# Routed attention and a gated spectral convolution: three-bank transposes, sums split between VectorE and GpSimd, and a new order of work

## The chip, the cores and the metric

The kernel runs on one core of a Trainium2 chip. The core has five engines that each work through a queue of their own in order: TensorE (PE in the profile; its weight loads are listed as PEld), VectorE (DVE), ScalarE (ACT), GpSimd (POOL) and SyncE (SP), which here only issues DMAs. They wait for each other through semaphores. Matrix products land in PSUM, eight banks of 128 partitions by 512 f32; all else lies in SBUF. The metric is the device time of one execution, the median of several.

## The reference

The first half is attention with a mask by clusters, for 4 batches, 8 heads, 768 positions and 64 columns per head. Each query and each key is assigned to one of 16 centroids of its head, and a query sees only the keys of its own centroid:

```
q_assign = argmax(q_n @ c_n.T)          # per head, over 16 centroids
k_assign = argmax(k_n @ c_n.T)
mask     = q_assign[:, None] == k_assign[None, :]
scores   = where(mask, q @ k.T / 8, -1e9)
attn     = softmax(scores)              # over the keys
x        = (attn @ v) with the heads side by side   # 768 x 512 per batch
```

The second half, per batch, multiplies two projections of `x` with a long convolution of the third, done in the frequency domain:

```
x1, x2, x3 = split(x @ w_proj)
x2_conv    = irfft(rfft(x2) * rfft(filter))     # along the 768 positions
out        = (x1 * x2_conv * x3) @ w_out
```

## The kernel before, in words

Attention goes by pairs of heads. There are 16 pairs (`n` is a group of two pairs, `NG` = 8; `pr` the pair in it), and each pair runs over six chunks `sk` of 128 keys. A chunk has 768 queries of two heads, so 1536 columns of scores, made in thirds of 512 columns (`THIRDS`): a score product into one PSUM bank (`sc`), an exponential on ACT into one of five buffers `p` (`exp`, lines 669 and 672). Then the chunk's product with the values is added into the pair of banks 4 and 5, `pair` (`pv`, line 683, f32), and the chunk's exponentials are added on VectorE into `acc` (line 697), whose sum over partitions gives the softmax denominators. The first sum of a pair takes chunks 0 and 1 together, the other four one chunk each, all 128x1536 f32. When the pair is done ACT copies `pair` to `osb` (line 701). The denominators of the middle ten pairs are reduced by three DMAs on GpSimd's queue that add one half of the partitions of `acc` onto the other (line 731), then go through DRAM (`dd`, `dp`, `dn`, `dr`) and return broadcast as `rb`; those of the first four pairs and of the last two use a product with ones on PE (`den`, line 711). Line 777 multiplies `osb` with `rb` into `xT`.

Ahead of a group, `routing` prepares its scores. The raw q and k (`qkraw`, six tiles of 128x128 f32 for a pair's q or k) are transposed on PE. From the third group on (`n > 1`), six transposes go into two banks in one go (`tr2`, line 556), and two copies of 384 columns bring them to `qkT`; the first two groups do three transposes per bank (line 566). The copies may go to ACT or VectorE (line 261 if ACT, line 263 if VectorE or GpSimd, both in the helper `copy`). `qkT` is cast to bf16 into `aug` (64x768, four casts for a pair), multiplied with the centroids (`sim`, line 586), transposed back (line 599), and VectorE makes one-hot rows of the nearest centroid (lines 607 to 624). These return through a transposing DMA as extra rows of `aug` (line 462), so that the score product itself carries the mask.

After every two groups a batch's `hyena` runs: the projection of x2 (line 809), a sum and a difference on VectorE (line 822), the spectrum (through `columns`), its products with the filter's spectrum from PSUM (`tm`, line 833), sums of those into `y` (line 837), the two other projections (`G`) with their product on VectorE (line 873), the inverse transform (`I`), its sums and differences into `sd` (line 898), their last sums into `yy`, called folds here (line 908), the product with the gate into `y2` (line 911), and the output projection (`W`), whose PSUM results are copied to `ob` and stored. For the first three batches this lies among the next attention groups, for the last it is the end of the kernel. On PE, `product` issues a 128-column product either whole (line 72) or as two halves of 64 columns (line 74), whichever keeps the array at the width of the instruction before.

The order of all this is not written by hand. Each step is an `op` with the engines that it may go to and a cost for each, a due time, what it reads and writes, and the banks that it takes and frees. `Plan.place` lists them: at each step it takes, of the engines' ready steps, the one that can start first, and among those within 0.1 us the one with the earliest due time; at most four banks may be held by scores, and at most four by other work, while scores last (`HELD`). A step marked `lock` on VectorE and one on GpSimd are never put beside each other. `NUDGE` adds a shift to the due time of single steps, by their number. The result is one fixed order on each engine; on the chip only the semaphores decide when each instruction starts.

The lines that say how a step meets its engine are few:

```
op(("DVE", 1.75), acc, due + .2 - 40 * (last and sk == NT - 1), ..., w=[("acc", os)], lock=True)
op({"POOL": 1.45, "DVE": .68} if last and i < 2 else ("DVE", .68), ...)      # y
op(("DVE", .55), fold, due + 2, ...)
op(("DVE", .95), ..., op=Alu.mult), due + 2.5, ...)                          # y2
```

Of the kernel before, what the change touches and what calls it, by code (L numbers as in the profile page):

```python
# [34 lines left out]
ROWS = 16  # L35
# [5 lines left out]
NUDGE = {6:-0.2,9:0.7,10:3.7,11:-0.3,71:-0.3,75:-1.5,90:7.4,91:7.4,129:-0.8,140:0.4,152:2.6,155:-6.2,156:6.6,158:-2.3,167:0.6,169:-4.1,187:-5.6,193:0.1,204:0.1,207:-0.7,209:0.8,212:-0.2,216:15.5,218:8.0,222:-3.8,228:-3.1,238:-1.7,239:-1.7,240:-1.7,243:1.1,245:-2.9,253:-4.1,255:-7.1,256:-7.1,257:-3.0,264:4.3,274:2.3,281:0.9,288:9.1,289:11.6,298:0.6,322:-4.8,328:-9.2,329:-0.5,343:0.7,363:0.5,368:-1.5,369:-1.5,370:0.7,371:-1.5,375:0.1,378:0.5,379:0.7,390:-1.8,391:-0.1,400:-0.2,406:2.8,409:-4.8,410:0.5,416:0.2,418:-1.0,433:-11.9,434:0.6,440:-3.7,479:0.8,480:-0.3,481:-0.5,485:1.1,494:-0.6,495:-4.2,504:2.3,508:-1.9,511:-0.2,517:-0.3,518:-5.0,523:-0.4,524:0.5,526:2.1,539:-2.3,547:0.2,554:10.5,558:0.3,565:-0.3,568:1.6,573:0.4,587:-4.9,590:0.2,595:-17.3,597:-2.4,617:0.7,620:-1.0,631:0.3,634:2.8,646:0.7,658:0.8,664:0.1,665:-1.9,684:2.2,690:-8.8,693:2.2,698:0.1,703:-7.8,704:-1.7,705:-1.7,729:0.5,740:1.0,750:-0.6,759:0.5,767:0.4,779:-0.7,782:1.7,784:-0.1,788:0.7,789:-0.3,790:0.8,800:2.5,805:-3.5,810:1.5,822:0.1,824:0.1,826:-0.5,828:-0.3,843:-8.5,848:-1.7,861:0.5,870:2.5,871:2.5,872:-1.3,883:-5.3,888:-3.6,897:-0.8,898:-1.1,901:-3.5,915:-3.1,926:4.0,936:-4.1,937:-3.0,940:2.9,941:0.4,947:-0.4,949:-0.6,969:-0.8,981:1.0,996:2.0,997:2.0,999:-0.3,1026:2.7,1029:-2.1,1031:0.1,1036:3.2,1039:2.0,1043:-1.2,1048:1.2,1050:-0.1,1054:-1.5,1056:10.8,1062:0.4,1066:0.9,1077:-7.7,1083:-3.4,1092:-0.1,1098:-1.0,1101:0.3,1116:-6.9,1118:-4.2,1122:2.8,1123:2.4,1124:2.4,1127:1.5,1130:-1.5,1131:0.3,1132:-2.9,1143:-2.6,1150:4.6,1157:-0.6,1194:-0.9,1236:-2.9,1253:-0.5,1255:0.7,1257:0.7,1263:0.3,1270:-0.2,1271:-1.1,1276:-3.6,1285:2.1,1286:4.6,1295:4.9,1311:-2.5,1317:-2.0,1321:0.4,1322:0.7,1332:-1.9,1337:-0.6,1351:5.6,1357:0.2,1359:0.5,1363:-0.5,1373:-1.5,1374:1.1,1381:0.2,1383:-0.3,1414:-2.7,1419:-0.5,1422:0.3,1425:0.7,1441:9.4,1450:3.5,1461:2.0,1478:-1.3,1479:3.3,1500:1.2,1501:-8.3,1521:0.2,1529:0.8,1546:0.2,1551:-0.2,1552:-1.1,1555:1.4,1557:0.1,1563:-0.6,1591:0.2,1600:-0.4,1619:-4.8,1624:2.8,1630:-1.5,1634:0.3,1640:-4.0,1641:-4.0,1642:-13.7,1643:-4.0,1655:-4.1,1657:0.4,1666:0.5,1672:1.9,1677:-0.3,1680:2.8,1681:2.8,1682:2.8,1685:-2.9,1697:-0.5,1713:-7.0,1741:5.6,1747:13.3,1764:1.1,1771:-3.3,1774:3.4,1776:0.2,1788:-7.8,1797:0.1,1808:-0.1,1809:-0.1,1814:-4.0,1817:-2.0,1823:3.3,1827:-0.7,1841:-1.3,1844:0.9,1859:2.4,1862:2.5,1863:2.1,1865:-0.3,1870:-0.4,1887:2.4,1890:3.2,1898:-7.4,1901:-0.8,1902:-1.5,1903:-0.8,1904:-0.8,1905:-1.8,1906:-1.8}  # L41
# [35 lines left out]
class Plan:  # L77
# [35 lines left out]
    def place(self, free0, banks_for, switch=0.1, wait=0.1, rate=215e3, bonus=10.84378, margin=0.02195, shape=1.63806):  # L113
# [57 lines left out]
        for o in self.ops:  # L171
            if not o.left:
                enqueue(o)
# [70 lines left out]
def build(T):  # L244
# [33 lines left out]

    def dma(e):
        return (T.nc.scalar if e == "ACT" else T.nc.sync).dma_start  # L280
# [4 lines left out]
    EV384 = {"ACT": .48, "DVE": .55}  # L285
# [89 lines left out]
    def tables(got):  # L375
# [44 lines left out]
        for i in range(3):  # L420
# [7 lines left out]
            for n, (row, c0, c1, cs) in enumerate(terms):  # L428
# [9 lines left out]
                op(("DVE", .68), lambda e, i=i, row=row, c0=c0, t=t, h=hs[1 - cs]: T.nc.vector.scalar_tensor_tensor(  # L438
# [28 lines left out]
    def first_masks(pr):  # L467
# [4 lines left out]
        for ch in range(2):  # L472
# [6 lines left out]
            op(("PE", .67), sim, due + .1 * ch, r=[("qkT", z, ch) for z in (2 * pr, 2 * pr + 1)] + ["cbd"], w=[h],  # L479
# [57 lines left out]
    def routing(n):  # L537
# [5 lines left out]
        for u in range(8):  # L543
# [7 lines left out]
            if n > 1 and ch == 0:  # L551
                h = Bank(cls, 2)

                def tr2(e, s=s, h=h):
                    for i in range(NT):
                        T.nc.tensor.transpose(bank(h.ids[i // 3])[:, ts(i % 3, 128)], raw(s, i), T.ident)  # L556
                op(("PE", .68), tr2, due, r=[("qkraw", s, 0), ("qkraw", s, 1), "ident"], w=[h], alloc=h)
                for c in range(2):
                    op(EV384, lambda e, z=z, c=c, h=h: copy(e, T.qkT[z][:, c], bank(h.ids[c])[:, :384]), due + .9,
                       r=[h], w=[("qkT", z, c)], free=[h])  # L560
            elif n < 2:
                h = Bank(cls)

                def tr(e, s=s, ch=ch, h=h):
                    for t in range(3):
                        T.nc.tensor.transpose(ap(h)[:, ts(t, 128)], raw(s, 3 * ch + t), T.ident)  # L566
                op(("PE", .36), tr, due, r=[("qkraw", s, 0), ("qkraw", s, 1), "ident"], w=[h], alloc=h)
                op(EV384 if n != 1 else {"ACT": .48}, lambda e, z=z, ch=ch, h=h: copy(e, T.qkT[z][:, ch], ap(h)[:, :384]),
                   due + .6, r=[h], w=[("qkT", z, ch)], free=[h])
            if ch == 1:  # L570
                for hp in range(2):
                    op({"ACT": .83, "DVE": .5, "POOL": .85} if n < 1 else {"ACT": .83, "DVE": .5}, lambda e, a=ring(n, pr), hp=hp, j=j, z=z: copy(
                        e, T.augs[a][hp][j][64 * hp:64 * hp + 64],
                        T.qkT[z][64 * hp:64 * hp + 64].rearrange("p a b -> p (a b)")), due + 8 if n else due + 6,
                       r=[("qkT", z, 0), ("qkT", z, 1), ("zero", ring(n, pr), j)],
# [12 lines left out]
        op(("PE", 1.33), sim, b0, r=[("qkT", z, ch) for z in range(4) for ch in range(2)] + ["cbd"], w=[h], alloc=h,  # L588
# [12 lines left out]
        op(("PE", .68), simT, b0 + 2.5, r=SIM + ["ident"], w=[h], alloc=h)  # L601
# [20 lines left out]
        op(("DVE", .85), largest, b0 + 4.1, r=both("oh"), w=both("m2"), lock=True)  # L622
# [15 lines left out]
    def attention(n, pr, sins):  # L638
# [8 lines left out]
        for sk in range(NT):  # L647
# [4 lines left out]
            for u in range(3):  # L652
# [20 lines left out]
                ex = op(("ACT", .61), exp, a + .5 + .25 * u, r=[h], w=[("p", s, u)],  # L673
# [13 lines left out]
            op(("PE", 1.347), pv, due, r=[("p", slots[sk], u) for u in range(3)] + [("vraw", vs), "eps"] +  # L687
               ([ob] if sk else []), w=[ob], alloc=None if sk else ob, kind="pv")
            todo = {1: [(0, 1)]}.get(sk, [(sk,)] if sk else [])
            if False:  # L690
                todo = []
                op(("POOL", .8), lambda e, sk=sk: T.nc.gpsimd.dma_start(
                    T.acc[os], T.p[slots[sk]][:, :, :S], accum_op=Alu.add), due - 3, r=PK(sk), w=[("acc", os)], byts=1150e3, lat=1.5)
            for t in todo:
                def acc(e, t=t):
                    P_ = lambda x: T.p[slots[x]][:, :, :S]
                    T.nc.vector.tensor_tensor(T.acc[os], P_(t[0]), P_(t[1]) if len(t) == 2 else T.acc[os], op=Alu.add)  # L697
                op(("DVE", 1.75), acc, due + .2 - 40 * (last and sk == NT - 1), r=sum(map(PK, t), []),
                   w=[("acc", os)], lock=True)
        te = A(i0 + NT) + 2.0 - 40.0 * last  # L700
        op(("ACT", .83), lambda e: T.nc.scalar.copy(T.osb[o3], two(ob)[:, :, :385]), te, r=[ob], w=[("osb", o3)],  # L701
# [474 lines left out]
```

## Time and profile before

| what | us |
|---|---|
| median of 3 runs | 387.17 (386.8 to 388.34) |
| the profiled execution, first to last instruction | 385.4 |
| PE busy | 367.3 |
| VectorE busy | 352.3 |
| ScalarE busy | 273.1 |
| GpSimd busy | 46.6 |

The profiled execution's span is 1.8 us below the median of the runs, which are timed around it. Busy times are the time in which at least one instruction of that engine was under way; on PE the records overlap, because products are pipelined, so its busy time hides short waits. GpSimd is busy almost only in the first 24 us, where it fills constants, and with the issue of its DMAs. The granted clock of TensorE was 0.998 over the span. The first transpose starts at 5.1 us, the first value product at 25.5 us and the last pair's first at 324.5 us; the last product ends near 381 us.

### The profile page before, as it was taken

The page shows a single profiled execution, that of the slowest core. Times are in us where ns is not written, and L with a number is a line of the kernel's source. Part 1 is how long each engine was busy: PE and PEld are TensorE (multiplying, and loading weights), DVE is VectorE, ACT ScalarE, POOL GpSimd, SP SyncE. Part 2 cuts the span into 40 slices and gives each one's busy share as a digit, 9 for nine tenths or more (in the row PEclk, how much of TensorE's full clock was granted, in tenths as well). Part 3 has the DMA queues.
Part 4 walks back from the last instruction along what each step waited for, and adds up shares of the span by engine and source line. Part 5 has one row for each costly group of instructions (what it writes and reads, how often), then busy time and mean ns, then how long its engine had stood idle before and what let it go on. Part 6 is the DMA issues. An engine that isn't in the chain of part 4 may idle for free.

```text
span 385.4 us, 8486 instructions
## 1 busy us (share of the span) xinstructions
PE 367.3 (95%) x3262; PEld 207.6 (54%) x3267; DVE 352.3 (91%) x504; ACT 273.1 (71%) x519; POOL 46.6 (12%) x92
## 2 busy tenths in 40 slices
PE   2999899999999999989999999999999999999995
PEld 1564345445655555556555555555455566555682
DVE  8898988998798999998899999999998999999883
ACT  5897987887894979577975967687867367532342
POOL 8602000000012010101010100101010100000400
PEclk9999999999999999999999999999999999999999
DMA  9819984730679669767886896645657551010214
GB/s 176 196 52 216 215 182 120 170 72 22 166 146 187 119 119 143 121 113 126 161 104 174 144 246 108 119 88 91 102 102 198 62 115 43 4 43 2 101 67 163
DMA packets 93860, 47.17 MB, mean 122 GB/s; under 512 B 82088, under 2 KB 87676, under 8 KB 93820
## 3 DMA queue, kind: packets, MB, share of 16 engines
q1 hardware_dynamic: 87836, 36.84, 42.5%
q0 software_dynamic: 2704, 8.98, 16.0%
q10 hardware_dynamic: 3280, 0.82, 1.2%
q8 instruction: 25, 0.41, 0.5%
q14 instruction: 15, 0.12, 0.1%
HBM read 31.59 MB, written 7.40 MB: 101 GB/s over the span
## 4 chain that ended last, share of the span: by engine, by line
PE 65%; DVE 19%; ACT 6%; issue 4%; DMA 3%; SPq 1%; POOL 0%; DVEq 0%; ACTq 0%; POOLq 0%
PE bank L74 24%; PE pair L683 21%; DVE acc L697 6%; PE bank L809 5%; PE bank L72 4%; PE bank L556 3%; ACT p L672 2%; PE bank L586 2%; DMA dr<-dn 2%; DMA aug<-ohT 2%; ACT aug L261 2%; DVE tm L833 2%; PE bank L599 1%; PE bank L451 1%; PE bank L566 1%
## 5 line engine op out<-in xcount | busy, mean ns | idle before, releaser
L683 PE MATMUL pair<-p,vraw 128*64 128x385 f32 x768 | 142.5, 490 | 0.2
L672 ACT ACTIVATE p<-bank 128x512 f32<-128x512 f32 x192 | 113.7, 613 | 34.1 <-PE bank L74 29.3
L697 DVE TENSOR_TENSOR acc<-p,acc 128x1536 f32<-128x1536 f32 x64 | 112.0, 1750 | 3.9 <-ACT p L672 1.5
L683 PEld LDWEIGHTS pair<-p,vraw 128*64 128x64 f32 x768 | 54.2, 136 | 47.8 <-issue 41.1
L74 PE MATMUL bank<-aug,aug 128*64 128x512 bf16 (+3 forms) x580 | 68.4, 328 | 2.1 <-ACT p L672 1.2
L669 ACT ACTIVATE p<-bank 128x512 f32<-128x512 f32 x96 | 58.6, 611 | 6.2 <-PE bank L74 5.6
L74 PEld LDWEIGHTS <-aug 128*64 128x64 bf16 (+1 forms) x580 | 34.4, 109 | 34.5 <-issue 22.4
L731 POOL DMA_DIRECT2D acc<-acc x30 | 23.6, 788 | 242.6 <-DMA acc<-acc 90.3
L74 PE MATMUL bank<-xT,wpj 128*64 128x384 bf16 x440 | 42.7, 326 | 0.0
L261 ACT COPY qkT<-bank 128x384 f32<-128x384 f32 x63 | 28.1, 497 | 10.5 <-PE bank L74 8.9
L74 PEld LDWEIGHTS <-wpj 128*64 128x64 bf16 x440 | 25.5, 109 | 15.9 <-issue 6.4
L697 DVE TENSOR_TENSOR acc<-p,p 128x1536 f32<-128x1536 f32 x16 | 28.0, 1751 | 3.3 <-ACT p L672 3.1
L74 PEld LDWEIGHTS <-y 128*64 128x64 bf16 x464 | 22.9, 110 | 12.6 <-issue 4.4
L261 ACT CAST aug<-qkT 64x768 bf16<-64x768 f32 x33 | 27.3, 829 | 2.5 <-PE bank L74 1.7
L833 DVE TENSOR_TENSOR tm<-bank,hm 128x512 f32<-128x512 f32 x44 | 27.7, 678 | 0.1
L809 PE MATMUL bank<-wpj,xT 128*64 128x512 bf16 x192 | 21.9, 379 | 0.0
L74 PE MATMUL bank<-wout,y 128*64 128x512 bf16 x176 | 21.1, 379 | 0.0
L72 PE MATMUL bank<-aug,aug 80*128 80x256 bf16 (+3 forms) x92 | 20.0, 321 | 0.2
L556 PE MATMUL bank<-ident,qkraw 128*128 128x128 f32 x144 | 19.6, 279 | 0.3 <-DVE sd L898 0.3
L556 PEld LDWEIGHTS bank<-ident,qkraw 128*128 128x128 f32 x144 | 15.6, 140 | 6.9 <-issue 4.5
L261 ACT COPY tm<-bank 128x512 f32<-128x512 f32 x13 | 7.4, 589 | 15.8 <-PE bank L809 12.0
L701 ACT COPY osb<-pair 128x770 f32<-128x770 f32 x16 | 12.9, 809 | 6.9 <-PE pair L683 6.8
(150 smaller groups left out, 433.0 us busy)
## 6 DMA issues: line engine op xcount, KB each, us to landing
vraw<-in_v_dram SPq DMA_DIRECT2D x16, 384.0 KB, 4.3
qkraw<-in_q_dram SPq DMA_DIRECT2D x30, 192.0 KB, 4.1
qkraw<-in_k_dram SPq DMA_DIRECT2D x30, 192.0 KB, 4.1
rb<-dr SPq DMA_DIRECT2D x30, 192.0 KB, 3.7
out_dram<-ob SPq DMA_DIRECT2D x11, 512.0 KB, 3.0
acc<-acc POOLq DMA_DIRECT2D x10, 384.0 KB, 6.2
acc<-acc POOLq DMA_DIRECT2D x10, 192.0 KB, 4.2
y<-in_moe_filter_fft_dram SPq DMA_DIRECT2D x4, 384.0 KB, 7.1
```

What stands on the lines that cost most here:

```text
L72: return T.nc.tensor.matmul(out, lhsT, rhs, start=start, stop=stop)
L74: T.nc.tensor.matmul(out[64 * i:64 * i + 64], lhsT[:, 64 * i:64 * i + 64], rhs, start=start, stop=stop)
L261: T.nc.scalar.copy(out, in_)
L556: T.nc.tensor.transpose(bank(h.ids[i // 3])[:, ts(i % 3, 128)], raw(s, i), T.ident)
L669: T.nc.scalar.activation(o, ap(h).rearrange("p (a b) -> p a b", a=2), Act.Exp, scale=0.125)
L672: T.nc.scalar.activation(flat(s)[:, lo:lo + 512], ap(h), Act.Exp, scale=0.125)
L683: T.nc.tensor.matmul(o[64 * hp:64 * hp + 64, ch, :385], T.vraw[vs][:, hp, sk * D:(sk + 1) * D], T.p[slots[sk]][:, hp, 384 * ch:384 * ch + ...
L697: T.nc.vector.tensor_tensor(T.acc[os], P_(t[0]), P_(t[1]) if len(t) == 2 else T.acc[os], op=Alu.add)
L701: op(("ACT", .83), lambda e: T.nc.scalar.copy(T.osb[o3], two(ob)[:, :, :385]), te, r=[ob], w=[("osb", o3)], free=[ob])
L731: op(("POOL", .8), lambda e, rows=rows: T.nc.gpsimd.dma_start(flat_()[:rows], flat_()[rows:2 * rows], accum_op=Alu.add), te, r=[], w=[("ac ...
L809: T.nc.tensor.matmul(ap(h)[64 * i:64 * i + 64], T.xT[xs][:, kt, c:c + 64], T.wpj[:, kt, DM:2 * DM], start=kt == 0, stop=kt == ND - 1)
L833: op(("DVE", .68), lambda e, i=i, cs=cs, r=r, h=h: T.nc.vector.tensor_tensor(T.tm[r][:, cs], ap(h), hmrow(i, (0, 2, 2, 3)[2 * r + cs]), op ...
```

## The change

Five things change at once.

Transposes of groups `n > 1`: one step transposes a pair's q and k together, twelve tiles into three banks, and three copies of 512 columns bring them to a joint tile `qkP`, of which `qkT` are now views. The casts to `aug` may go to GpSimd in all groups.

First sums of exponentials: the addition of chunks 0 and 1 is split into the same thirds as the exponentials, each of 128x512, on VectorE or GpSimd.

In `hyena`, the sums into `y` may go to GpSimd in all batches, and for all batches but the last also the folds and the product into `y2`.

The planner's costs are changed in many places, by a few hundredths of a us to two tenths.

`NUDGE` is replaced by a table with 1,840 entries for 271 before, so one for nearly every step, and with values up to thousands of us, so that it sets the order almost alone. A new table `ONLY` binds 234 steps that may go to several engines to one of them.

```diff
-NUDGE = {6:-0.2,9:0.7,10:3.7,...}
+NUDGE = {0:-2.65714,1:-0.164318,2:15.6428,3:104.959,...}
+ONLY = {23:"SP",24:"SP",25:"SP",26:"ACT",...}
...
+        for o in self.ops:
+            if o.seq in ONLY:
+                o.eng = {ONLY[o.seq]: o.eng[ONLY[o.seq]]}
...
-            if n > 1 and ch == 0:
-                h = Bank(cls, 2)
-                def tr2(e, s=s, h=h):
-                    for i in range(NT):
-                        T.nc.tensor.transpose(bank(h.ids[i // 3])[:, ts(i % 3, 128)], raw(s, i), T.ident)
-                op(("PE", .68), tr2, due, ...)
-                for c in range(2):
-                    op(EV384, lambda e, z=z, c=c, h=h: copy(e, T.qkT[z][:, c], bank(h.ids[c])[:, :384]), due + .9, ...)
+            if n > 1 and z % 2 == 0 and ch == 0:
+                h = Bank(cls, 3)
+                ss = [qslot[n, pr, x] for x in range(2)]
+                def tr2(e, ss=ss, h=h):
+                    for i in range(2 * NT):
+                        T.nc.tensor.transpose(bank(h.ids[i // 4])[:, ts(i % 4, 128)], raw(ss[i // NT], i % NT), T.ident)
+                op(("PE", 1.42), tr2, due, ...)
+                for c in range(3):
+                    op(EV512, lambda e, pr=pr, c=c, h=h: copy(e, T.qkP[pr][:, ts(c, 512)], bank(h.ids[c])), due + 1.6, ...)
...
-                    op({"ACT": .83, "DVE": .5, "POOL": .85} if n < 1 else {"ACT": .83, "DVE": .5}, lambda e, ...: copy(
+                    op({"ACT": .82, "DVE": .65, "POOL": .95}, lambda e, ...: copy(
                         e, T.augs[a][hp][j][64 * hp:64 * hp + 64], ...
...
-            for t in todo:
-                def acc(e, t=t):
-                    P_ = lambda x: T.p[slots[x]][:, :, :S]
-                    T.nc.vector.tensor_tensor(T.acc[os], P_(t[0]), P_(t[1]) if len(t) == 2 else T.acc[os], op=Alu.add)
-                op(("DVE", 1.75), acc, due + .2 - 40 * (last and sk == NT - 1), ..., w=[("acc", os)], lock=True)
+            AK = [("acc", os, u) for u in range(3)]
+            if sk == 1:
+                for u in range(3):
+                    def part(e, u=u):
...
+                        alu(e).tensor_tensor(o, x, y, op=Alu.add)
+                    op({"DVE": .63, "POOL": 1.5}, part, due - 1 + .2 * u, r=[("p", slots[i], u) for i in range(2)], w=[("acc", os, u)], lock=True)
+            if sk > 1:
+                def acc(e, sk=sk):
+                    T.nc.vector.tensor_tensor(T.acc[os], T.p[slots[sk]][:, :, :S], T.acc[os], op=Alu.add)
+                op(("DVE", 1.75), acc, due + .2 - 40 * (last and sk == NT - 1), r=PK(sk), w=AK, lock=True)
...
-                op({"POOL": 1.45, "DVE": .68} if last and i < 2 else ("DVE", .68), lambda e, i=i, r=r: alu(e).tensor_tensor(
+                op({"POOL": 1.5, "DVE": .68}, lambda e, i=i, r=r: alu(e).tensor_tensor(
                     T.y[:, i, r], T.tm[r][:, 0], T.tm[r][:, 1], op=Alu.add if r else Alu.subtract), due + 2, ...
...
-                op(("DVE", .55), fold, due + 2, ...
+                op(("DVE", .55) if last else {"DVE": .55, "POOL": 1.2}, fold, due + 2, ...
...
-            op(("DVE", .95), lambda e, dt=dt, x3=x3, yy=yy: alu(e).tensor_tensor(
+            op(("DVE", .95) if last else {"DVE": .95, "POOL": 2.1}, lambda e, dt=dt, x3=x3, yy=yy: alu(e).tensor_tensor(
                 T.y2[:, dt], ...
...
-    T.qkT = [tl([128, 2, 384], F32, f"qkT{i}") for i in range(4)]
+    T.qkP = [tl([128, 2 * S], F32, f"qkP{i}") for i in range(2)]
+    T.qkT = [T.qkP[i // 2][:, S * (i % 2):S * (i % 2) + S].rearrange("p (a b) -> p a b", a=2) for i in range(4)]
```

More of the change, by code (lines that the diff above doesn't have):

```diff
@@ L277, in two, with qk @@
         return T.pair[2]
+    def qk(z, ch):
+        return [("qkT", z, i) for i in (((0,), (1, 2)), ((0, 1), (2,)))[z % 2][ch]]
     def dma(e):
@@ L283, in alu @@
         return T.nc.vector if e == "DVE" else T.nc.gpsimd
-    EV384 = {"ACT": .48, "DVE": .55}
+    EV384 = {"ACT": .465, "DVE": .55}
     EV512 = {"ACT": .585, "DVE": .68}
@@ L478, in sim @@
                                        start=True, stop=True)
-            op(("PE", .67), sim, due + .1 * ch, r=[("qkT", z, ch) for z in (2 * pr, 2 * pr + 1)] + ["cbd"], w=[h],
+            op(("PE", .67), sim, due + .1 * ch, r=[x for z in (2 * pr, 2 * pr + 1) for x in qk(z, ch)] + ["cbd"], w=[h],
                alloc=h, kind="sim")
@@ L587, in sim @@
                                        T.qkT[z][:, ch], start=True, stop=True)
-        op(("PE", 1.33), sim, b0, r=[("qkT", z, ch) for z in range(4) for ch in range(2)] + ["cbd"], w=[h], alloc=h,
+        op(("PE", 1.43), sim, b0, r=[x for z in range(4) for ch in range(2) for x in qk(z, ch)] + ["cbd"], w=[h], alloc=h,
            kind="sim")
@@ L621, in largest @@
                 x = y
-        op(("DVE", .85), largest, b0 + 4.1, r=both("oh"), w=both("m2"), lock=True)
+        op(("DVE", 1.07), largest, b0 + 4.1, r=both("oh"), w=both("m2"), lock=True)
         for j, o_ in ((1, Alu.is_equal), (0, Alu.subtract)):
@@ L686, in pv @@
                                            start=(sk == 0), stop=(sk == NT - 1))
-            op(("PE", 1.347), pv, due, r=[("p", slots[sk], u) for u in range(3)] + [("vraw", vs), "eps"] +
+            op(("PE", 1.3), pv, due, r=[("p", slots[sk], u) for u in range(3)] + [("vraw", vs), "eps"] +
                ([ob] if sk else []), w=[ob], alloc=None if sk else ob, kind="pv")
[L689 to L693, printed above, removed]
@@ L845, in hyena @@
             if last:
-                x3, xkeys = (lambda dt=dt: T.qkT[dt][:]), [("qkT", dt, ch) for ch in range(2)]
+                x3, xkeys = (lambda dt=dt: T.qkT[dt]), [qk(dt, ch) for ch in range(2)]
             else:
-                x3, xkeys = (lambda xb=dt % 2: T.x3[xb][:]), [("x3", dt % 2, ch) for ch in range(2)]
+                x3, xkeys = (lambda xb=dt % 2: T.x3[xb][:]), [[("x3", dt % 2, ch)] for ch in range(2)]
             if last and dt % 2:
```

55 lines of the change are left out of this document (31 added, 24 removed).

## The prediction

> **What bounds the kernel now.** I read the page's busy line first, then the sums by stretch, the chain in order of time, the rows of the groups that the change touches, and last two stretches of the timeline where GpSimd works beside VectorE.
>
> ```profile
> span 385.4 us, 8486 instructions
> PE 367.3 (95%) x3262; PEld 207.6 (54%) x3267; DVE 352.3 (91%) x504; ACT 273.1 (71%) x519; POOL 46.6 (12%) x92
> PE 65%; DVE 19%; ACT 6%; issue 4%; DMA 3%; SPq 1%; POOL 0%; DVEq 0%; ACTq 0%; POOLq 0%
> 24.00:160.00 136.00, 133.24 (x1060) 70.15 (x1062) 123.63 (x161) 112.10 (x213) 9.86 (x14) 1.00 0.70 138
> 160.00:265.00 105.00, 103.11 (x887) 58.71 (x887) 100.07 (x136) 79.66 (x154) 11.75 (x15) 1.00 0.72 138
> 265.00:357.00 92.00, 91.02 (x878) 52.60 (x878) 89.07 (x131) 53.24 (x101) 6.35 (x8) 1.00 0.37 73
> ```
>
> Columns of the last three: stretch, length, then busy time of PE, PEld, DVE, ACT and POOL. From 24 to 357 us PE has no idle time worth the name, and DVE idles 12.4 + 4.9 + 2.9 = 20.2 us. Two engines are full, so the chain weaves between them:
>
> ```profile
> 37.89 0.83 ACT aug L261
> 38.73 0.83 ACT aug L261
> 39.58 0.83 ACT aug L261
> 40.42 0.83 ACT aug L261
> 128.49 1.29 PE pair L683 x8
> 129.78 0.81 PE bank L556 x6
> 132.74 1.45 PE pair L683 x8
> 137.22 1.46 PE bank L556 x12
> 164.30 1.76 DVE acc L697
> 167.82 1.01 DVE xT L777
> 168.84 0.94 DVE sd L898 x2
> ```
>
> PE's busy time overstates its work, since the records of matmuls overlap. Counting each matmul by the shortest step from its start to the next one's gives 347 us of work (a value product 1.29, a score third 0.22, a transpose 0.109, and so on). Between 24 and 357 us the starts show 20.0 us beyond those steps: 7.4 in 66 changes of the array's column width (0.11 each, which the value product at 1.45 behind transposes shows against 1.29), 3.0 in crumbs, and 9.6 in 18 longer waits. The longest: 1.7 at 39.6 (behind the four casts on ACT above), 0.9 at 162.0 (behind an x3 product on DVE that stands behind sums of exponentials), 0.9 at 338.8 and 0.7 at 90.5 (denominators waiting for the last sum), 0.65 at 168.7 (a bank that DVE's sd has not freed). The other 18 us: 5.1 before the first transpose, about 4 more before 24 us, 4.4 from the last matmul to the end, and the rest changes of width outside that stretch. What can be won is 9.6, some of the early 4, and a few changes of width.
>
> **The change, part by part.**
>
> ```profile
> L697 DVE TENSOR_TENSOR acc<-p,p 128x1536 f32<-128x1536 f32 x16 | 28.0, 1751 | 3.3 <-ACT p L672 3.1
> L837 DVE TENSOR_TENSOR y<-tm 128x512 bf16<-128x512 f32 x20 | 13.0, 679 | 0.0
> L837 POOL TENSOR_TENSOR y<-tm 128x512 bf16<-128x512 f32 x4 | 5.1, 1276 | 50.8 <-DVE tm L833 50.8
> L261 ACT COPY qkT<-bank 128x384 f32<-128x384 f32 x63 | 28.1, 497 | 10.5 <-PE bank L74 8.9
> 5.88 1.95 DVE L350 TENSOR_SCALAR ob<-ob 128x384 f32<-128x384 f32 x2
> 6.81 0.81 POOL L987 MEMSET aug<- 64x768 bf16 x1
> 356.10 2.53 POOL L837 TENSOR_TENSOR y<-tm 128x512 bf16<-128x512 f32 x2 [50.08 <-DVE tm L833]
> 357.60 1.87 DVE L833 TENSOR_TENSOR tm<-bank,hm 128x512 f32<-128x512 f32 x3
> ```
>
> Counts after the change come from the order of its instructions; durations from the rows of before.
>
> First sums. 16 whole additions go (-28.0). Of 48 thirds 26 stay on DVE; a 128x512 addition is not in the trace from two f32 tiles to f32, and the nearest row is y's 0.679: +17.7. 22 thirds go to GpSimd at y's 1.276: 28.1 there. A whole sum on DVE as thirds costs 2.04 for 1.75, so the gain is only in what leaves DVE.
>
> Gate sums, folds, products. 13 of 20 y sums leave DVE (-8.8), 9 of 24 folds (-4.9), one product (-1.0). On GpSimd: 13 x 1.276 = 16.6; a fold isn't shown there, and lies between 0.96 (y's by elements) and 1.28, I take 0.96: 8.6; the product by elements 1.9.
>
> Casts of q and k into aug. DVE 27 to 11 (-16 x 0.574 = -9.2), ACT 33 to 31 (-1.7), GpSimd 4 to 22 (18 x 0.82 = 14.8).
>
> Transposes. As many matmuls as before; twelve in one go instead of twice six. Three evictions of 512 for four of 384: ACT 63 copies to 20 of 384 and 27 of 512 (0.59, the row of ob): -5.4. DVE 9 to 4 and 9 of 512 (0.69): +3.7. The program's changes of width fall from 85 to 77: 8 x 0.11 = -0.9 on PE, which is on the path.
>
> Choices of engine, now fixed. DVE takes 5 more evictions of ob, 5 of od, 4 of sim, 4 of x, and small ones: +11.7. ACT gives them: about -10.5.
>
> Sums: DVE -28.0 + 17.7 - 8.8 - 4.9 - 1.0 - 9.2 + 3.7 + 11.7 = -18.8, to 333.5. ACT -17.6, to 255.5. GpSimd +70.0, to 117. PE the same 347, less 0.9.
>
> What GpSimd's work does to DVE. The two f32 scalings at L350 took 0.98 and 1.05 with GpSimd memsets running, 0.35 without; with the like of it at L348, L320 and a cast (1.06 for 0.56), DVE lost 3.2 us to GpSimd's 14.5 busy us before 24 us: 0.22 per us. At 356 us the products from PSUM (1.87 for three) ran untouched beside GpSimd's sums. So only instructions that work SBUF to SBUF are held. By the tail the added 70.0 us cost 0, by the head 15.4. The order after stands many GpSimd sums beside DVE's PSUM readers, but 64 DVE additions of 1.75 us remain to collide with: I take half, 7.7, and keep both ends. DVE then ends at 341, 11 us below before. The GPSIMD Engine Reference of the Trainium skill (Specifications) says that GpSimd's SBUF interfaces are shared with VectorE and contend with its instructions of two SBUF inputs or in a two-port mode. Head and tail agree with it; read as a meeting every time, it would cost the whole 70.0 us, where the rows give 0 to 15.4.
>
> The queue on GpSimd. Its 30 reduction DMAs stay, each waiting for the last to land (90.3 us of waiting, up to 6.6 at a time). In the new order thirds, folds and casts stand between the steps. A third behind such a step comes up to 6.6 late; behind it wait the next DVE sum, then the exponentials that reuse p. p has five buffers, and a pair of six chunks takes 16 to 20 us but where hyena stands between, so near 3 us each, which covers one such delay: I cost it at 0, up to 2 us in a few pairs if the cover is gone. In the other direction a step behind a third is 1.3 late; its chain (dd, dp, dn, dr, rb) ends in xT, read only by the next projection.
>
> SP, and the head. SP issues the same 236 items, in another order at the margin. The first transposes need two loads that were issued side by side on SP (0.69 us) and ACT; both now stand on SP, in a row: up to 0.6 late, or nothing where landing sets it. I take +0.3.
>
> Three banks at once. A twelve holds three of the six free banks for 1.3 + 0.6 us at least, against two for 0.8 + 0.5. Where ACT is late a score third waits; 12 such groups, 0 to 0.6 each: 0 to 7, I take 1, because ACT is lighter.
>
> **The sum.** The 1.7 at 39.6 goes whole, because those casts leave ACT (-1.7). The other 7.9 of PE's waits stand against 20.2 us of DVE slack; with 11 us more slack I scale them by 20.2/31.2 to 5.1 (-2.8). Widths -0.9, SP +0.3, banks +1.0, and -0.5 of the 4 us before 24 us, where casts leave ACT and DVE too: -4.6 in all, from 385.4 to 380.8 of span. The profiled execution stands 1.8 below the median of 387.17 (what lies around the span, with its scatter), so 382.6; I say 382.
>
> **The rivals.**
> All waits go, because slack is what PE lacked and holds are near 0: 387.2 - 9.6 - 0.9 - 2 early = 374.7. For it: DVE is 96% full from 160 to 357. Against: the waits at 251 (a mask's DMA) and at 90 and 338 (last sums) don't hang on load.
> Nothing moves: PE is full at 347 and its widths, and other waits take the place: 387.2 - 0.9 = 386.3. For it: PE idles under 1% in its page rows.
> GpSimd holds DVE, the slower side. Place: the 1.75 us sums from 160 to 357, where DVE is full. It decides from 18.8/70.0 = 0.27 us held per us of GpSimd on; the head showed 0.22. At 0.37, 26 us held, DVE ends 7 above before in a stretch without slack, and PE follows: 387.2 + 7 - 0.9 = 393. Against it: the tail's zero. The GPSIMD Engine Reference of the Trainium skill (Engine selection) keeps two-input elementwise work on VectorE, as about twice as slow on GpSimd; by the rows it is 1.276 for 0.679.
> Banks, slower too: 12 x 0.6 = 7 lost and half the gain kept: 387.2 + 7 - 2.3 = 392. For it: ACT's exponentials idled 29.3 us for PE's scores before, so a score that waits for a bank is felt on ACT at once. Against it: ACT is the lightest of the three full engines, and evicts within its 0.59.
>
> **How the numbers follow.** Forecast (378 to 385) 0.42, first rival 0.18, second 0.14, third 0.19, fourth 0.07. A measurement of this kernel tells about 0.5% (1.9 us) from no change. Faster holds the forecast and the first, 0.60; same the second, 0.14; slower the last two, 0.26. The range runs from the first rival's 374.7, less 1.7 for a smoother head, to just under the slower two, of which about a half is left out: 373 to 392. The forecast's own is 378 to 385.
>
> **What would show it.** DVE busy 335 to 345, ACT near 256, POOL near 117; DVE sums at 1.75 with few stretched over 2.0 (right), or many at 2.5 to 3 (the third rival); PE's waits for DVE shorter, and no ACT casts in the chain near 40 us; value products at 1.45 fewer. I am wrong if DVE gets lighter by 19 and the time stays (the second), if exponentials idle more for PE in the middle (banks), or if GpSimd's sums wait behind its DMA steps and DVE waits for them.

## The result, and the profile after

The changed kernel takes 400.5 us (median of four runs, 397.6 to 403.5) where the kernel before takes 387.8 beside it: a ratio of 1.033, 95% interval 1.027 to 1.040. I had forecast 382.0, in a range that ended at 392, and gave "slower" 0.26. The change costs 13 us. Some executions of any kernel here run some per cent longer than its others; the ratios leave them out, and so does the time given for e8 below (400.0 and 401.6 count, 409.9 and 412.8 do not). The granted clock explains little of the 13 us: over the four executions of the changed kernel it was 0.987 to 1.0, and the one at 1.0 took 398.8 us.

The profiled execution took 402.3 us, of which its span is 400.5. The page of the changed kernel, first line, busy line and shares of the chain:

```profile
span 400.5 us, 8667 instructions
PE 370.5 (93%) x3343; PEld 221.7 (55%) x3343; DVE 358.5 (90%) x497; ACT 259.5 (65%) x483; POOL 132.9 (33%) x155
PE 41%; DVE 31%; issue 9%; DMA 8%; ACT 6%; SPq 2%; ACTq 1%; DVEq 0%; POOL 0%; POOLq 0%
```

VectorE was to lose work and has more busy time than before (352.3); its share of the chain goes from 19% to 31%. The same three stretches (columns as before: PE, PEld, DVE, ACT, POOL):

```profile
24.00:160.00 136.00, 127.56 (x1002) 66.19 (x1002) 116.36 (x140) 102.69 (x188) 38.62 (x35) 0.99 0.72 133
160.00:265.00 105.00, 97.79 (x874) 56.84 (x872) 99.92 (x137) 69.14 (x129) 39.03 (x35) 1.00 0.70 131
265.00:357.00 92.00, 90.11 (x862) 57.81 (x860) 88.37 (x114) 56.58 (x106) 32.02 (x26) 1.00 0.45 89
```

PE now idles 17.5 us in these stretches, even by its overlapping records, where it idled 5.6. Counted as in the prediction (each matmul by its shortest step), PE's starts show 34.2 us beyond the steps between 24 and 357 us, for 20.0: 25.6 in 27 waits of over 0.2 us (9.0 in 15 before; the prediction's 9.6 in 18 has three shorter ones in it), 6.2 in changes of width (7.8 before) and 2.4 in crumbs. The work itself, 347 us, is the same. So the loss is waits, and most of them end with VectorE. The groups that show why, with the mean duration in ns behind the busy time:

```profile
L713 DVE TENSOR_TENSOR acc<-p,acc 128x1536 f32<-128x1536 f32 x64 | 118.8, 1856 | 6.3 <-ACT p L681 1.9
L709 POOL TENSOR_TENSOR acc<-p,p 128x512 f32<-128x512 f32 x22 | 32.8, 1493 | 24.7 <-ACT p L681 11.8
L267 POOL CAST aug<-qkP 64x768 bf16<-64x768 f32 x22 | 26.3, 1200 | 64.1 <-ACT qkP L265 35.0
L852 POOL TENSOR_TENSOR y<-tm 128x512 bf16<-128x512 f32 x17 | 23.9, 1413 | 22.5 <-DVE tm L848 20.2
L923 POOL TENSOR_TENSOR yy<-sd 128x384 f32<-128x384 f32 x9 | 12.9, 1459 | 27.2 <-DVE sd L913 23.1
```

A sum that took 1750 ns takes 1856 in the mean, and GpSimd's own work is longer too: its casts took 898 ns before. I call *held* the time by which a VectorE instruction exceeds the median of its shape by over 0.1 us while GpSimd has an instruction under way. Before, 2.6 us were held, all of it in the first 24 us; after, 26.0 us in 32 places: 12.9 by thirds, 4.7 by y sums, 4.1 by folds, 2.8 by casts. Three places in the timeline:

```profile
111.70 2.11 DVE L792 SCALAR_TENSOR_TENSOR xT<-osb,rb 128x768 bf16<-128x768 f32 x1
111.72 1.27 POOL L709 TENSOR_TENSOR acc<-p,p 128x512 f32<-128x512 f32 x1 [1.44 <-ACT p L681]
...
126.53 4.05 DVE L713 TENSOR_TENSOR acc<-p,acc 128x1536 f32<-128x1536 f32 x2
127.78 1.19 POOL L267 CAST aug<-qkP 64x768 bf16<-64x768 f32 x1 [1.72 <-ACT qkP L265]
130.50 1.27 DVE L848 TENSOR_TENSOR tm<-bank,hm 128x512 f32<-128x512 f32 x2
131.81 0.41 PE L75 MATMUL bank<-aug,aug 80*64 80x512 bf16 x2 [2.31 <-DVE tm L848]
...
205.51 2.13 DVE L621 TENSOR_TENSOR oh<-oh,revx 128x768 bf16<-128x768 bf16 x1
205.69 1.53 POOL L709 TENSOR_TENSOR acc<-p,p 128x512 f32<-128x512 f32 x1
```

xT takes 1.01 us alone and 2.11 beside a third; the masks' product oh 0.56 alone and 2.13. The held time (1.10, 1.57) is about the whole of the GpSimd instruction (1.27, 1.53), so the two do not share, one stands. The "SBUF — State Buffer" page of the Trainium skill (SBUF: two separate sides) says that the port pair that both use is an exclusive lock, which whichever starts first holds for the whole instruction. These rows agree that the two do not share. They do not bear out who goes first: by its record VectorE starts first in both, by 0.02 and 0.18 us, and it is VectorE that is held. In the second place two sums take 4.05 us for 3.5, the product tm behind them starts late, and PE waits 2.3 us, by the profile for tm (the masks came late there too, as the part on the load of w_out shows).

### The profile page after: what moved, and what is told of

Read it like the earlier page. It is cut to its first block, busy times and chain, and to the rows that moved or that the text cites. A ratio compares the mean times of both kernels' runs of the same rounds, so it can differ in the third digit from the quotient of the medians.

```text
span 400.5 us, 8667 instructions
## 1 busy us (share of the span) xinstructions
PE 370.5 (93%) x3343; PEld 221.7 (55%) x3343; DVE 358.5 (90%) x497; ACT 259.5 (65%) x483; POOL 132.9 (33%) x155
## 4 chain that ended last, share of the span: by engine, by line
PE 41%; DVE 31%; issue 9%; DMA 8%; ACT 6%; SPq 2%; ACTq 1%; DVEq 0%; POOL 0%; POOLq 0%
PE bank L75 19%; PE pair L692 12%; DVE acc L713 9%; PE bank L824 3%; DVE tm L848 2%; DMA dd<-acc 2%; PE bank L73 2%; DVE x L888 2%; SPq L469 2%; DMA acc<-acc 2%; PE bank L564 1%; DVE uv L425 1%; DVE xT L792 1%; DVE yy L923 1%; DMA ohT<-oh 1%
## 5 line engine op out<-in xcount | busy, mean ns | idle before, releaser
L713 DVE TENSOR_TENSOR acc<-p,acc 128x1536 f32<-128x1536 f32 x64 | 118.8, 1856 | 6.3 <-ACT p L681 1.9
L75 PE MATMUL bank<-aug,aug 128*64 128x256 bf16 (+3 forms) x652 | 72.2, 329 | 6.8 <-DVE tm L848 2.9
L75 PEld LDWEIGHTS <-aug 80*64 80x64 bf16 (+1 forms) x652 | 40.5, 110 | 41.3 <-issue 30.6
L267 POOL CAST aug<-qkP 64x768 bf16<-64x768 f32 x22 | 26.3, 1200 | 64.1 <-ACT qkP L265 35.0
L709 POOL TENSOR_TENSOR acc<-p,p 128x512 f32<-128x512 f32 x22 | 32.8, 1493 | 24.7 <-ACT p L681 11.8
L265 ACT COPY qkP<-bank 128x512 f32<-128x512 f32 (+1 forms) x47 | 23.7, 541 | 17.5 <-PE bank L75 9.4
L852 POOL TENSOR_TENSOR y<-tm 128x512 bf16<-128x512 f32 x17 | 23.9, 1413 | 22.5 <-DVE tm L848 20.2
L265 ACT CAST aug<-qkP 64x768 bf16<-64x768 f32 x31 | 25.7, 830 | 1.7 <-DVE qkP L267 0.5
L709 DVE TENSOR_TENSOR acc<-p,p 128x512 f32<-128x512 f32 x26 | 19.0, 749 | 4.3 <-DMA dd<-acc 2.1
L923 POOL TENSOR_TENSOR yy<-sd 128x384 f32<-128x384 f32 x9 | 12.9, 1459 | 27.2 <-DVE sd L913 23.1
L716 ACT COPY osb<-pair 128x770 f32<-128x770 f32 x16 | 12.9, 804 | 10.6 <-PE pair L692 10.5
```

The lines of the kernel that those rows point to most:

```text
L75: T.nc.tensor.matmul(out[64 * i:64 * i + 64], lhsT[:, 64 * i:64 * i + 64], rhs, start=start, stop=stop)
L265: T.nc.scalar.copy(out, in_)
L267: (T.nc.vector if e == "DVE" else T.nc.gpsimd).tensor_copy(out, in_)
L709: alu(e).tensor_tensor(o, x, y, op=Alu.add)
L713: T.nc.vector.tensor_tensor(T.acc[os], T.p[slots[sk]][:, :, :S], T.acc[os], op=Alu.add)
L852: op({"POOL": 1.5, "DVE": .68}, lambda e, i=i, r=r: alu(e).tensor_tensor(T.y[:, i, r], T.tm[r][:, 0], T.tm[r][:, 1], op=Alu.add if r else ...
```

## The experiments

The theories. *Holds*: GpSimd's SBUF work stretches VectorE's instructions, and the time follows. *Lateness*: GpSimd's results come late, because a sum takes 1.3 us and more there for 0.7, in a queue with the reduction steps. *Order*: the new order with its three-bank transposes is worse on the chip, whatever GpSimd does. Later *load*: one DMA issued ahead of another. Time is the median; held and PE's waits (those over 0.2 us between 24 and 357 us) are from the one profiled execution of each kernel, which lies up to 3.4 us from its median, and are counted as above.

| kernel | time, us | ratio to before, 95% interval | DVE busy | held | PE's waits |
|---|---|---|---|---|---|
| before | 387.1 to 387.8 | | 352.3 | 2.6 | 9.0 in 15 |
| changed | 400.5 | 1.027 to 1.040 | 358.5 | 26.0 | 25.6 in 27 |
| e1 sums cut short | 390.9 | 1.005 to 1.010 | 339.2 | 7.4 | 12.9 in 18 |
| e2 short, but late | 391.4 | 1.007 to 1.014 | 338.9 | 4.8 | 15.4 in 20 |
| e3 short, idle work behind | 394.7 | 1.016 to 1.021 | 347.9 | 16.1 | 15.5 in 21 |
| e4 before, with idle work | 397.0 | 1.020 to 1.027 | 363.7 | 12.9 | 19.1 in 21 |
| e5 changed, load later | 398.3 | 1.020 to 1.038 | 357.1 | 26.4 | 21.3 in 28 |
| e6 before, load earlier | 387.6 | 0.996 to 1.002 | 352.3 | 2.6 | 9.3 in 17 |
| e7 thirds on VectorE | 399.1 | 1.016 to 1.033 | 357.1 | 14.1 | 23.7 in 24 |
| e8 casts on ScalarE | 400.0, 401.6 | 1.022 to 1.042 | 353.4 | 20.3 | 24.8 in 38 |
| e9 short, load later | 388.7 | 0.999 to 1.005 | 338.8 | 7.0 | 7.7 in 13 |
| e10 sums on VectorE, load later | 395.2 | 1.014 to 1.026 | 360.0 | 4.5 | 20.2 in 26 |
| e11 before, two casts on GpSimd | 388.4 | 0.998 to 1.005 | 352.5 | 2.9 | 11.3 in 14 |
| e12 before, with tiny memsets | 387.0 | 0.997 to 1.001 | 352.0 | 2.6 | 9.5 in 11 |

**Three kernels in the changed order: neither, lateness alone, holds.** All keep the order and every wait, and leave out most of GpSimd's sums, which they make in 8 columns only. The emission differs in what `alu("POOL")` does:

```diff
+        def tensor_tensor(self, o, x, y, op):
...
+            for _ in range(self.before):                 # e2: 14
+                T.nc.gpsimd.memset(T.idle[:1, :1], 0.0)
+            T.nc.gpsimd.tensor_tensor(few(o), few(x), few(y), op=op)   # 8 columns
+            for _ in range(self.after):                  # e3: 3
+                T.nc.gpsimd.tensor_tensor(T.idle[:], T.idle[:], T.idle[:], op=Alu.mult)
-        return T.nc.vector if e == "DVE" else T.nc.gpsimd
+        return T.nc.vector if e == "DVE" else Brief(0, 0)
```

> The changed kernel in its own order, with 57 of GpSimd's two-input sums and products (all but the first three thirds) cut to the first 8 columns of each row; the casts, the reduction steps and every wait stay, and seven small zeroing copies on ScalarE (4 us in all) stand in for what is no longer written. The sums of exponentials, gate sums and products are thus left out in part. It takes some 64 us of GpSimd's work away. Holds theory (GpSimd's SBUF work stretches VectorE's SBUF instructions: 26.0 us held in the changed kernel): held time falls to 3 to 5, VectorE to 334 to 338 busy, time 376 to 385. Lateness theory (GpSimd's results come late, since they take 1.4 us for 0.7 and stand behind reduction steps): the same 376 to 385, but with VectorE's busy time not the reason. Order theory (the new order and the three-bank transposes are themselves worse on the chip, whatever GpSimd does): 395 to 402.

(There are 46 such sums and products, not 57, and GpSimd's busy time falls by 51 us to 81.5.) Measured 390.9: 9.6 us of the 13 go with them, but the kernel is not faster than before, although VectorE's busy time falls to 339.2. No theory had this number. Holds or lateness carry most of the loss, and something else carries 3 us.

> As the kernel with 8-column sums, but each of the 57 is preceded on GpSimd by 14 memsets of one element (some 90 ns each, 1.25 us in all), so that the result comes as late as in the changed kernel and the queue is as full, while SBUF is hardly touched. Holds theory: held time stays at 3 to 6 us and the time within 4 us of the 8-column kernel. Lateness theory: back at 396 to 402 with VectorE's own durations as short as in the 8-column kernel. Order theory: both kernels 395 to 402.

Measured 391.4, 0.5 us above e1 with intervals that overlap, at 141.6 us of GpSimd busy time. Late results and a full queue cost nothing that can be measured: lateness falls.

> As the kernel with 8-column sums, but each of the 57 is followed on GpSimd by three two-input products of 128x160 f32 on a tile that nobody else reads (1.2 to 1.3 us in all): SBUF is as busy and the queue as full as in the changed kernel, but the results are early. Holds theory: held time 18 to 28 us, time 394 to 402. Lateness theory: held or not, 376 to 388, since nobody waits for these products except the next step in the queue. Order theory: 395 to 402.

Measured 394.7, with 8.7 us more held than in e1 (less than I had expected) and 3.8 us more time. Nobody reads the idle products. Holds alone make the kernel slower, at about 0.44 us of time for each held us; from e1 to the changed kernel it is 9.6 us for 18.6 held, 0.52.

**The same in the order of before.** e4 adds 45 triples of idle products to the kernel before, and e12, its control, the same places with 14 tiny memsets each.

```diff
+    then = 24.0
...
         o.fn(o.on)
+        if o.kind == "exp" and then < o.start < 352:
+            for _ in range(3):          # e12: 14 times nc.gpsimd.memset(T.idle[:1, :1], 0.0)
+                nc.gpsimd.tensor_tensor(T.idle[:], T.idle[:], T.idle[:], op=Alu.mult)
+            then = o.start + 5.9
```

> The kernel before, its order and its work unchanged, with 55 idle triples of two-input 128x160 f32 products on GpSimd, one about every 5.9 us from 24 to 352 us (some 70 us of GpSimd work on a tile that nobody reads; the output stays the reference's). Holds theory at the price seen in the changed kernel (0.37 us held per us): 20 to 28 us held, VectorE 372 to 380 busy where PE and it have 20 us of slack: 392 to 402. My prediction's middle value (0.11 per us): 8 held, 387 to 390. Lateness theory and order theory: no result is later except reduction steps by up to 1.3 us, 386 to 389.

> The control for the idle products: the kernel before, its work and output unchanged, with 14 memsets of one element at each of the 45 places where the idle triples stood (45 x 14 x 95 ns = 60 us of GpSimd's time, reduction steps behind them as late, SBUF hardly touched). Holds theory: VectorE 352 to 354 busy, time 386.5 to 388.5. If the idle triples cost their 9.6 us by making the reduction steps late: 392 or more.

GpSimd's costliest group, first in e4, then in e12 (busy us, mean ns, idle time before):

```profile
L1151 POOL TENSOR_TENSOR idle<-idle 128x160 f32<-128x160 f32 x135 | 102.8, 762 | 8.2
```

```profile
L1151 POOL MEMSET idle<- 1x1 f32 x630 | 63.4, 101 | 34.5
```

There were 45 places, not the 55 of the expectation, and the products took 103 us for the 70 that I had counted, because GpSimd is held too. An idle product takes 0.44 us alone and 0.76 here. With 63 us of tiny memsets nothing happens (387.0): reduction steps that come later by 1.4 us at each place are not the cause (a held triple makes it 2.3, which has no control). With the idle products VectorE is held 10.3 us more, its busy time grows by 11.4, PE's long waits by 10.1, and the time by 9.6. The held time per GpSimd us is 0.10, the middle value of my prediction; what was wrong is what I made of it. VectorE idled 20.2 us in these stretches, and I had let such an addition disappear in there. It came through nearly whole.

The holds of e4 are 42 of 0.24 us in the mean (24 to 357 us), those of the changed kernel 29 of 0.86: the idle products are short, a third or a y sum is 1.28 long. The price of a meeting goes up to the length of GpSimd's instruction.

**The other three microseconds: the load of w_out.** In e1, as in the changed kernel, PE waits long between 129 and 133 us (the wait at 128 us of the expectations below). In the changed kernel the profile names tm as the last releaser; in e1, with nothing held there, it names the masks:

```profile
132.80 0.41 PE L75 MATMUL bank<-aug,aug 80*64 80x512 bf16 x2 [2.70 <-DMA aug<-ohT]
```

The SP queue ahead of it, first before, then changed:

```profile
114.21 1.27 SPq L629 DMA_TRANSPOSE ohT<-oh  x1
115.54 0.58 SPq L295 DMA_DIRECT2D qkraw<-in_k_dram  x1
116.17 0.62 SPq L301 DMA_DIRECT2D vraw<-in_v_dram  x1
117.10 6.03 SPq L462 DMA_DIRECT2D aug<-ohT  x8
```

```profile
116.60 1.27 SPq L638 DMA_TRANSPOSE ohT<-oh  x1
117.92 0.87 SPq L308 DMA_DIRECT2D vraw<-in_v_dram  x1
125.40 5.01 SPq L469 DMA_DIRECT2D aug<-ohT  x8
```

The masks wait for the transposing transfer, 2.9 us before, 8.8 after. The load of w_out is issued at 115.86 before, behind that transfer, and at 114.56 after, ahead of it. e5 issues it behind the masks in the changed kernel, e6 ahead of the transfer in the kernel before.

```diff
...
+    turn = [i for i, o in enumerate(order) if o.kind == "mask"]
+    i = next(i for i, o in enumerate(order) if o.byts == 1048e3)
+    order.insert([j for j in turn if j > i][7], order.pop(i))        # e5, e9
```

```diff
+    i = next(i for i, o in enumerate(order) if o.byts == 1048e3)    # e6
+    turn = order.index(next(order[j] for j in range(i, 0, -1) if order[j].kind == "turn"))
+    load = order.pop(i)
...
+    def early(e, fn=load.fn):
+        nc.gpsimd.tensor_copy(T.tick, T.mt[0:1, 0:4])
+        fn(e)
+    load.fn = early
+    order.insert(turn, load)
```

> The changed kernel with one move: the load of w_out (1 MB on GpSimd's queue) is issued behind the eight mask transfers of the fourth group of heads (about 130 us) and not at 114.6 us, 2.0 us ahead of the transposing transfer of the one-hot words. In the changed kernel and in the 8-column kernel that transfer is followed by the first mask only 8.8 and 9.5 us later, against 2.9 in the kernel before, which issues the load 1.7 us behind it; TensorE then waits 2.5 to 2.9 at 128 us. Load theory (the big load stands in the transfer's way): masks 3 to 5 us after the transposing transfer, TensorE's wait at 128 us under 0.5, time 396.5 to 399. Theory that the wait is VectorE's lateness: the wait stays over 2, time 399.5 to 402.

> The kernel before, its output unchanged, with the load of w_out issued ahead of the same transposing transfer and not behind it (a copy of four elements of the largest words holds it until about 112.5 us). Load theory: masks 6 to 10 us after the transposing transfer for 2.9, TensorE waits 1 to 3 us more at about 124 to 128 us, time 388 to 390. Otherwise 386.5 to 388.

The queue of e6:

```profile
114.53 1.41 SPq L629 DMA_TRANSPOSE ohT<-oh  x1
115.98 0.58 SPq L295 DMA_DIRECT2D qkraw<-in_k_dram  x1
116.62 0.69 SPq L301 DMA_DIRECT2D vraw<-in_v_dram  x1
122.62 5.94 SPq L462 DMA_DIRECT2D aug<-ohT  x8
```

In e5 the masks follow 3.2 us after the transposing transfer (8.8 before the move) and the wait at 128 us is gone; the time, 398.3, lies 2.2 below the changed kernel's, but the intervals overlap. In e6 they follow 8.1 us after, so the load does delay the transfer; the time stays at 387.6, presumably because there the first reader is not due yet. The mechanism is right and its price hangs on the cover; my expectation of 1 to 3 us for e6 was wrong.

> The 8-column kernel (57 of GpSimd's sums and products cut to 8 columns, left out in part) and the late load of w_out together. If held time and the load are the whole of the loss: 387 to 389, TensorE's wait at 128 us under 0.5 (2.9 in the 8-column kernel). If the new order is worse in some further way: 390 to 392 again, with the wait turned up elsewhere.

Measured 388.7, ratio 1.002 (0.999 to 1.005), and PE's waits at 7.7 in 13. The load is worth 2.2 us from e1, and with it and the sums away the new order runs like the old one. In sum, of 13 us 9.6 go with GpSimd's sums and 2.2 with the load, and the rest can't be told from nothing. The busy line of e9 also tells what there was to win:

```profile
PE 367.7 (96%) x3343; PEld 229.3 (60%) x3343; DVE 338.8 (88%) x497; ACT 262.0 (68%) x490; POOL 83.5 (22%) x156
```

VectorE is 13.5 us lighter than before, ScalarE 11, and the time is the same (this profile is of e9's fastest execution, 385.6). That clears the new order only for so light a VectorE: either lighter work buys nothing, or it buys just what the new order costs. No run cuts the same sums short in the order of before, which would tell the two apart; e10 below speaks in part for the second.

**Parts taken back in the changed order.**

```diff
...
-        o.fn(o.on)
+        o.fn("DVE" if o.kind == "third" else o.on)                               # e7
+        o.fn("ACT" if o.kind == "cast" and o.on == "POOL" else o.on)             # e8
+        o.fn("DVE" if o.on == "POOL" and o.kind == "sum" and o.start < 350 else o.on)   # e10, with e5's move
```

> The changed kernel in its own order, with GpSimd's 22 thirds of first sums carried out by VectorE at the same place. VectorE gets 22 x 0.75 = 16.5 us of work and loses the 12.9 us by which thirds held it. Holds theory: VectorE's busy time 360 to 363, time 398 to 404, so that the move of the thirds to GpSimd had bought nothing. If GpSimd's slower results counted, or the move did spare VectorE, 394 to 397 or 405 to 410.

> The changed kernel in its own order, with the 18 casts of q and k that had come to GpSimd carried out by ScalarE at the same place (18 x 0.83 = 15 us more there, 259.5 to 275 of busy time, as before the change). Holds theory: the 2.8 us held by casts go, and so do some of the places where a cast makes GpSimd late for VectorE's next sum: 396.5 to 399.5. If ScalarE's time is short instead: exponentials late, 401 to 404.

> The changed kernel in its own order with the late load of w_out, and 45 of GpSimd's sums and products (all but those of the last 40 us) carried out by VectorE at the same place: 31 us more work on VectorE, some 22 of 26 us held gone. Holds theory at half a microsecond of time per microsecond of VectorE, as between the 8-column kernel and the changed one: VectorE 364 to 368 busy, 400 to 404. If work that VectorE was planned to do costs less than work that comes by surprise (holds come where the order did not count on them): 392 to 397.

e7: 399.1, VectorE 357.1 with 14.1 held. The time is as expected, VectorE's busy time 3 us below: the 22 thirds on GpSimd had bought nothing. (The profiled execution had a granted clock of 0.985; one at 0.996 took 394.3, so on VectorE the thirds may even be the faster.)

e8: VectorE gets 5.1 us lighter, and held time falls by about as much, 5.7 us, more than the casts' own 2.8, as the holds theory had it. Yet the time, 400.0 and 401.6, is that of the changed kernel. ScalarE has 13.3 us more work (272.8 for 259.5); that may have eaten the gain, but it is not shown.

e10: 45 sums more on VectorE, some 31 us of work, with its held time down to 4.5, and 395.2, 3.1 below e5 (the intervals overlap). VectorE's busy time is 3 us above e5's. Doing the work on VectorE is at least as fast as having it done on GpSimd. The time is below the 400 to 404 of half a microsecond per microsecond, and in the range of the other theory, that planned work costs less. But with the holds nearly gone and the load late, e10 is still 8 us slower than the kernel before, with VectorE 7.7 us busier. Whether that is the new order itself, or work that stands where the order had not planned it, no run separates; so the order does not fall as a theory for the kernel that does all its work.

**One wait of before.** e11 takes two of the four casts behind which PE waits at 39.6 us to GpSimd, in the kernel before.

```diff
+    some = [o for o in order if o.kind == "cast" and o.on == "ACT" and 30 < o.start < 44]
+    some = some[-2:]
...
+        o.fn("POOL" if o in some else o.on)
```

> The kernel before, its output unchanged, with two of the four casts that ScalarE does in a row at 37.9 to 41.3 us (behind which TensorE waits 1.7 us at 39.6) carried out by GpSimd at the same place. My prediction took this wait to go whole when those casts leave ScalarE: 385.5 to 386.3. If the wait is replaced by the next one (VectorE's last sum or the mask transfers behind it): 387 to 388.

Measured 388.4, no gain. The same place in its timeline:

```profile
38.87 0.60 ACT L672 ACTIVATE p<-bank 128x512 f32<-128x512 f32 x1
38.92 1.25 PE L74 MATMUL bank<-aug,aug 128*64 128x512 bf16 x12
39.56 1.75 DVE L697 TENSOR_TENSOR acc<-p,acc 128x1536 f32<-128x1536 f32 x1
41.46 0.85 PE L711 MATMUL bank<-acc,ones 128*32 128x384 f32 x8 [1.28 <-DVE acc L697]
```

The exponentials come 2.4 us earlier than before (38.87 for 41.27; the stretch ahead of them had begun 0.7 earlier), and PE then waits 1.28 us for the denominators' last sum on VectorE: 1.45 beyond its steps, for 1.69. No version in this study beats the kernel before by more than the noise.

## Why the prediction was wrong

Step by step, in its own terms.

- *VectorE's work, -18.8 to 333.5*: right. The changed kernel's 358.5, less 23.4 us held more than before, is 335.1. ScalarE was to be 255.5 and is 259.5. GpSimd was to be 117 and is 132.9, since it is held as well.
- *Holds, 7.7 of 0 to 15.4*: mis-sized, the first term that failed. 23.4 us more were held, for 70.0 us of added work 0.33 per us; the upper end, 0.22, came from memsets and short instructions in the head. A meeting costs up to a whole GpSimd instruction (0.86 us in the mean), and the added ones are long. Taking half was a place between two ends and rested on nothing.
- *PE's waits scale with VectorE's slack (7.9 to 5.1)*: wrong, and the larger fault. Had I put in the 23.4 us held, slack would have been 20.2 + 18.8 - 23.4 = 15.6 us, the 7.9 us of waits 10.2, and the forecast 387.7: still 12.8 below the measured time, of which the load of w_out explains 2.2. With holds away (e9) and VectorE 13.5 us lighter, PE's long waits are 7.7 for 9.0, and the time is no shorter (though the new order may have taken back what lighter work gave). In the other direction 20.2 us of idle VectorE absorbed under 2 of the 11.4 us that e4 adds. Idle time summed over a stretch is not slack: it lies where a queue waits for something else. That is argued; the two numbers are shown.
- *The 1.7 at 39.6 goes whole*: wrong in the order of before. e11 removed its cause, and VectorE's last sum took its place with 1.28. I had not asked what was late next.
- *Widths, -0.9*: right in kind. Changes of width fell by eight as counted, and cost 6.2 us for 7.8 between 24 and 357 us.
- *SP in the head, +0.3*: mis-sized. The first transpose starts at 6.41 for 5.11, 1.3 late, and both loads that it needs are now SP's, where one of them was ScalarE's.
- *Three banks, +1.0*: right. Scores wait 1.1 us in two places for VectorE to empty such a bank, and no other wait names them.
- *GpSimd's queue at 0*: right for results that come late (e2: 0.5, not told from nothing). Wrong in what I looked for there: the load of w_out passes the transposing transfer, 1.3 us earlier against 2.4 later, and costs 2.2 us (e1 to e9). I had compared SP's items among themselves and GpSimd's steps among themselves, not one against the other.

The third rival had the mechanism and nearly the amount: at 0.37 per us it named 26 us held, and 23.4 more were, 0.33 per us. The place was right in part: nearly three quarters of the held time lies from 160 to 357 us, but only a quarter of it on the 1.75 us sums; the rest fell on shorter instructions, the masks' products, the folds, the casts and the 128x12 additions. It gave 393, because it set the 18.8 us of work taken from VectorE against the holds, us for us. The runs do not show that this work bought any time (e9); without it, 23.4 us held more, at the 0.52 from e1 to the changed kernel, is 12, a price that this same kernel gave. The second rival, that nothing moves, said 386.3. e9 comes near it with 388.7, but without most of GpSimd's sums; e10, which makes all of them and is hardly held, takes 395.2.

## What to carry to other kernels

Work moved to GpSimd is paid for on VectorE by the meeting: count the VectorE instructions with two inputs in SBUF, and the casts and scalings from SBUF to SBUF, around it, and charge up to the length of GpSimd's instruction for each, not a share of its busy time. An engine's idle time is slack only if it lies where the new work falls; to learn what lighter work would bring, cut the work short in the order that you have, before moving it anywhere (e9 did so in the new order only, and so left the question half open). When an order is made anew, compare the DMA issues of all queues with one another, big loads against the small transfers that somebody waits for.

## What the runs showed of the hardware

- Where they met, VectorE and GpSimd excluded one another: the one-hot product of 0.56 us took 2.13 beside a third of 1.53. Even the smallest instruction pays it: the 128x12 addition behind the gathered denominators took up to 1.93 us for 0.17.
- Not every VectorE instruction was held: tm, which reads PSUM, took 0.69 us at 140.22 us inside a third of 1.27 us, and the reduction of the gathered denominators (one input, 128x192, SBUF to SBUF) 0.48 us at 322.42 beside a third of 1.28, both as long as alone.
- It works both ways. At 57.68 us a sum took its 1.76 us, and the cast beside it on GpSimd 2.20 for 0.82. GpSimd's casts went from 898 to 1200 ns in the mean, its thirds to 1493 from 1276 for the nearest row of before, and its idle products of 160 columns took 762 ns in e4 and 628 in e3.
- Memsets of one element held nothing: 630 of 101 ns on GpSimd left VectorE at 352.0 us. Whether that is because they are small or because they read nothing, no run separates.
- A transfer from one queue delays one from another: the load of w_out (1 MB read, 512 KB written, 9.9 us from issue to landing in the changed kernel), issued 1.0 to 2.0 us ahead of the transposing transfer, put the masks behind that transfer from 2.9 us to between 8.1 and 9.4.
